# Wave 1's second half turned by DMA transposes, smaller first loads and later side work in an attention + MLP kernel

## The chip, the cores and the metric

One core of a Trainium2 chip runs the whole kernel. The metric is the device time in microseconds, as the median over runs. In the profile, PE is TensorE (matmuls), PEld its weight loads, DVE is VectorE, ACT is ScalarE, POOL is GpSimd and SP is SyncE, whose queue (SPq) issues nearly every DMA here. The sixteen DMA engines of the core serve that queue.

## The reference, cut to what matters

The input is q, k, v of shape (4 batches, 8 heads, 768 positions, 64), one decay factor `lam` for each head, and two weight matrices. The result is a decayed linear attention, followed by a two-layer MLP.

```python
for b in range(nb):                       # blocks of 64 positions
    intra = einsum('bhic,bhjc->bhij', qb, kb) * Dmask
    intra = einsum('bhij,bhjd->bhid', intra, vb)
    inter = einsum('bhid,bhde->bhie', qb * lam_pow, kv_state)
    out[:, :, sl] = intra + inter
    kv_state = lam_block * kv_state + einsum('bhsd,bhse->bhde', kb * rev_pow, vb)
x = out.transpose(0, 2, 1, 3).reshape(3072, 512)
h = x @ w_in                              # 512 -> 2048
g = h * (1 / (1 + exp(-1.702 * h)))
return g @ w_out                          # 2048 -> 512
```

## The kernel before, in words

The 3072 rows are worked through in six waves of 512 rows. Each wave runs an attention part (small matmuls), then `mlp1` with `gelu` (16 column groups `fc`, four matmuls of 128x512 each), then `mlp2` (four row groups of 16 matmuls each). All products are in bf16.

Waves 0 and 1 hold the first 256 positions of two batches each, and are built of eight units (bl, p): a batch and a pair of heads. Waves 2 to 5 hold 128 positions of all four batches and are built of four pairs p. The score matmuls need k and q with the head dimension on partitions, so both must be transposed after they have been scaled and cast. In waves 0 and 1, for each unit:

- `u_cast_kq` (L264) scales k on DVE and q on POOL from the f32 ring into `kqs`; `u_cast_v` (L270 on ACT, L272 on POOL) casts v.
- `u_turn` (L281) transposes with four PE matmuls against the identity into PSUM, and `u_turn_copy` (L289 on ACT, L291 on DVE) copies that to `kq`.
- `u_score` (L302), `u_mask` (L307), `u_kv0` (L327) with `u_kv0_copy` (L336), `u_inter` (L361) and `u_out` (L370) with a copy into `xT` (L372) do the rest; `u_state` (L348, L351) makes the state for wave 2.

In waves 2 to 5, `p_cast` (L382, L384) feeds a DMA transpose through the crossbar (L386) instead, and `p_out` sends its result through another one into `xT` (L436).

All inputs go through one SBUF `ring` of 52 half slots. A load is put on the list `coming`, and `pump()` issues from the head of that list as slots come free. Loads of waves 0 and 1 are `load_units` (L89, packets of 512 bytes), weights are `load_w` (L117), loads of wave 2 and later are `load_batch` (L101, packets of 256 bytes). SP issues in program order, and a DMA also waits until the eighth DMA before it has landed.

From wave 0's MLP on, the order of the instructions is written by hand on a virtual clock. `put` places the MLP work (`main`; one `fc` of 512 columns is 1, a half one is 0.5, four matmuls of `mlp2` are 1). `at` places attention work, casts and loads (`side`). A side item is emitted ahead of the first main item whose clock is not below its own. Each engine then works its instructions off in that order. `A_UNITS` is the first half of wave 1 (bl 0), done during wave 0's `mlp1`; `B_UNITS` is the second half (bl 1), done during wave 0's `mlp2`. `A_T` and `A_S` are the start and the step of the first half. `states`, `full` and `load_spread` place `u_state`, the attention of waves 2 to 5, and their loads.

Of the kernel before, what the change touches and what calls it, by code (L numbers as in the profile page):

```python
# [24 lines left out]
def kernel(  # L25
# [13 lines left out]
    nc = tc.nc  # L39
    f32 = mybir.dt.float32  # L40
    bf16 = mybir.dt.bfloat16
    B, H, S, D = q.shape
# [43 lines left out]
    def load_units(w, nm, bl, p, n=2):  # L86

        def go(x):
            nc.sync.dma_start(  # L89
                out=x.rearrange("s (h c) -> s h c", h=2 * n),  # L90
                in_=SRC[nm][2 * w + bl, 2 * p : 2 * (p + n), 0 : 2 * P, :].rearrange("h (q j) d -> q h (j d)", j=2))
            for i in range(n):
                loaded[w, nm, bl, p + i] = x.rearrange("s (n h j d) -> s n h j d", n=n, h=2, j=2)[:, i]
        coming.append((n, [(w, nm, bl, p + i) for i in range(n)], 1, go))

    def load_batch(w, nm, b):

        def go(x):
            if b == 0:
                loaded[w, nm] = x.rearrange("s (b p h d) -> s b p h d", b=B, h=2, d=D)  # L100
            nc.sync.dma_start(out=loaded[w, nm][:, b].rearrange("s p h d -> s (p h) d"),  # L101
                              in_=SRC[nm][b, :, w * P : (w + 1) * P, :].rearrange("h s d -> s h d"))
        coming.append((2 * B if b == 0 else 0, [(w, nm)] if b == 0 else [], NP, go))

    def load_batches(w):
        for nm in "kqv":
            for b in range(B):
                load_batch(w, nm, b)

    def load_w(kind, j, r):  # L110

        def go(x):
            if kind == "in":
                src = moe_w_in[r * P : (r + 1) * P, j * W : (j + 1) * W]
            else:
                src = moe_w_out[(j * CW + r) * P : (j * CW + r + 1) * P, :]
            nc.sync.dma_start(out=x, in_=src)  # L117
            loaded[kind, j, r] = x
        coming.append((2, [(kind, j, r)], 1, go))

    def pump():

        while coming:
            n, keys, reads, go = coming[0]
            i = (head[0] + (head[0] % 2 if n > 1 else 0)) % (2 * NR)
            if n == 0:
                coming.pop(0)
                go(None)
                continue
            if i + n > 2 * NR:  # L130
                i = 0
            if any(c in used for c in range(i, i + n)):
                break
            m = n // max(1, len(keys))
            for a, key in enumerate(keys):
                where[key] = [range(i + a * m, i + (a + 1) * m), reads]
            used.update(range(i, i + n))
            head[0] = i + n
            coming.pop(0)
            go(ring[:, i : i + n, :].rearrange("s n c -> s (n c)"))  # L140
# [17 lines left out]

    UNITS = [(bl, p) for g in range(2) for bl in range(2) for p in (2 * g, 2 * g + 1)]
    A_UNITS, B_UNITS = [(0, p) for p in range(NP)], [(1, p) for p in range(NP)]  # L160
    for p in (0, 2):
        for bl in range(2):
            for nm in "kqv":
                load_units(0, nm, bl, p)
    for u in ROWS:
        load_w("in", *u)
    for bl in range(2):
# [3 lines left out]
        if bl == 0:  # L171
            for u in ROWS:
                load_w("out", *u)
    load_batches(2)
    pump()

    zeros = const.tile([P, W], bf16)
# [65 lines left out]
    kqs_of, kq_of, sm_of = {}, {}, {}  # L243
# [40 lines left out]
    def u_turn_copy(w, bl, p, eng):  # L284
        if (w, p) not in kq_of:
            kq_of[w, p] = work.tile([P, 2, 2, 2, P], bf16, tag=f"kq{p}", name="kq")
        t, out = t_ps.pop((w, bl, p)), kq_of[w, p][:, bl]
        if eng is nc.scalar:
            nc.scalar.copy(out, t)  # L289
        else:  # L290
            eng.tensor_copy(out, t)  # L291

    s_ps = {}

# [215 lines left out]

    FILL0, FILL = 12, (0, 2, 2, 2, 1, 1, 1, 1)
    NF = 3
    A_T, A_S = 6, 1.4
    KV_ENG = {i: nc.vector if i in (2, 4, 6) else nc.scalar for i in range(1, 9)}

    with tc.manual_schedule():
# [8 lines left out]
        for i in range(N + 2):  # L525
            u = UNITS[i] if i < N else None
# [16 lines left out]
            if u:  # L543
                fill(FILL[i])
                u_turn(0, *u)
                u_turn_copy(0, *u, nc.vector if i < 2 else nc.scalar)
# [26 lines left out]
        def put(length, *item):  # L573
            main.append((clock[0], item))
            clock[0] += length

        def at(t, *item):
            side.append((t, item))

        def units1(t0, units, step, vcast, copier):  # L580
            n = len(units)
            for i in range(n + 2):
                t = t0 + step * i
                h = t + 0.5 * step
                if i < n:
                    at(t, u_cast_kq, 1, 0, *units[i], nc.vector)
                    at(t, u_cast_kq, 1, 1, *units[i], nc.gpsimd)
                    at(t, u_cast_v, 1, *units[i], vcast)
                if 0 < i:
                    at(h, new_o)  # L590
                if i < n:
                    at(h, u_turn, 1, *units[i])
                if i > 1:
                    at(h, u_inter, 1, *units[i - 2])
                if i < n:
                    at(h, u_turn_copy, 1, *units[i], copier)
                if 0 < i <= n:
                    at(h, u_score, 1, *units[i - 1])
                    at(h, u_mask, 1, *units[i - 1])
                    at(h, u_kv0, 1, *units[i - 1])  # L600
                if i > 1:
                    at(h, u_out, 1, *units[i - 2])
                if 0 < i <= n:
                    at(h, u_kv0_copy, 1, *units[i - 1], nc.scalar)

        def states(t0, w, step):
            for p in range(NP):
                at(t0 + step * p, u_state, w, p)

        def full(t_cast, t0, w, step, c_step=2.0):  # L610
            for p in range(NP):
                at(t_cast + c_step * p, p_cast, w, p)
            for p in range(NP + 1):
                t = t0 + step * p
                if p < NP:
                    at(t, p_score, w, p)
                    at(t, p_mask, w, p)
                if p:
                    at(t, p_inter, w, p - 1)
                    at(t, p_out, w, p - 1)  # L620
                if p < NP:
                    at(t, p_kv, w, p)

        def load_spread(t0, w, step):
            for i, nm in enumerate("kqv"):
                for b in range(B):
                    at(t0 + step * (B * i + b), load_batch, w, nm, b)
# [10 lines left out]
        for fc in range(3, FFC):  # L638
            put(0.5, fc_whole, 1, fc, HA)
        for n, u in enumerate(ROWS):  # L640
            at(13.2 + 0.6 * n, cast_w, "out", *u, nc.vector)
        e = clock[0]
        for j in range(NJ):
            for g in range(3):
# [1 line left out]
        for j in range(NJ):  # L646
            put(1, mlp2, 0, 3, j)
        states(e - 7, 0, 1.6)
        units1(e + 2, B_UNITS, 2, nc.scalar, nc.scalar)
        e = clock[0]  # L650
        for fc in range(FFC):
            put(0.5, fc_whole, 1, fc, HB)
        states(e + 0.5, 1, 1.5)
        for g in range(G):
            for j in range(NJ):
                put(1, mlp2, 1, g, j)
        full(e + 1, e + 7.6, 2, 2.4)
        load_spread(e + 4, 3, 1.8)
        for w in range(2, NW):
            e = clock[0]  # L660
# [47 lines left out]
```

## Time and profile before

| | |
|---|---|
| median of 13 runs | 220.68 us (220.04 to 221.97) |
| the profiled execution's own time | 221.12 us |
| its span | 219.3 us |
| PE busy | 211.2 us (96% of the span), 1766 matmuls |
| DVE, ACT, POOL busy | 106.1, 97.1, 28.8 us |
| DMA moved | 40.15 MB, mean 183 GB/s |
| DMA engines' busy share, five-us stretches from 5 to 60 us | 1.01 to 1.28 |
| the same from 60 to 75 us | 0.66 to 0.73 |

A busy share is a sum over packets of all sixteen engines and can pass 1 where packets overlap, so values of 1 and more mean a full queue. PE is busy in all of every five-us stretch from 45 us to the end of the MLP; its idle time lies ahead of that. The span of a matmul is longer than its share of the pipeline: 128x512 matmuls follow each other every 0.216 us, and one `fc` or four matmuls of `mlp2` take 0.86 us at the full clock.

### The profile page before, as it was taken

How to read it: one execution, taken by the hardware profiler on the slowest of the kernel's cores; microseconds unless marked ns; L12 is line 12 of the kernel's file. 1: busy time of each engine (PE TensorE's matmuls, PEld its weight loads, DVE VectorE, ACT ScalarE, POOL GpSimd, SP SyncE). 2: the span in 40 equal slices, each digit the busy share in tenths (PEclk: the TensorE clock that was granted, in tenths of full speed). 3: DMA queues.
4: the chain of work that ended last, by engine and by line, in shares of the span. 5: the costliest groups of instructions: out<-in, count | busy, mean ns of one | idle time of the engine just before them, and what ended most of it. 6: DMA issues, size and time to landing. Idle time of an engine off the chain costs nothing.

```text
span 219.3 us, 4494 instructions
## 1 busy us (share of the span) xinstructions
PE 211.2 (96%) x1766; PEld 108.7 (50%) x1766; DVE 106.1 (48%) x237; ACT 97.1 (44%) x203; POOL 28.8 (13%) x62
## 2 busy tenths in 40 slices
PE   7899969899999999999999999999999999999994
PEld 2464425575546755444554444544444444444453
DVE  3896536584415889182573295671393432100120
ACT  3786727774765612155621066611166520367000
POOL 4773051040040000004000040000040000000000
PEclk9999988999999999999999999999999999999999
DMA  4999999999965999899979979878974132200112
GB/s 120 296 328 371 333 308 388 361 270 216 221 126 126 168 213 212 179 249 219 228 155 179 234 170 190 170 155 176 236 155 85 34 88 75 96 0 0 48 51 96
DMA packets 96693, 40.15 MB, mean 183 GB/s; under 512 B 77088, under 2 KB 89632, under 8 KB 96672
## 3 DMA queue, kind: packets, MB, share of 16 engines
q1 hardware_dynamic: 96528, 39.86, 76.9%
q8 instruction: 14, 0.23, 0.5%
q14 instruction: 7, 0.06, 0.1%
q10 hardware_dynamic: 144, 0.00, 0.0%
HBM read 27.27 MB, written 6.29 MB: 153 GB/s over the span
## 4 chain that ended last, share of the span: by engine, by line
PE 84%; DMA 8%; SPq 5%; ACT 1%; issue 0%; POOL 0%; DVE 0%
PE ps_out L485 36%; PE ps_h L454 35%; DMA ring<-in_moe_w_in_dram 5%; SPq L89 4%; DMA ring<-in_q_dram 3%; PE ps_o L432 2%; PE ps_s L395 2%; PE ps_out L501 2%; PE ps_kv L410 1%; PE ps_o L425 1%; PE ps_t L281 1%; PE ps_kv L348 1%; PE ps_s L302 1%; SPq L117 1%; PE ps_o L370 0%
## 5 line engine op out<-in xcount | busy, mean ns | idle before, releaser
L454 PE MATMUL ps_h<-xT,w_in 128*128 128x512 bf16 (+1 forms) x448 | 89.1, 352 | 0.3 <-ACT g_sb L460 0.3
L460 ACT ACTIVATE g_sb<-ps_h 128x512 bf16<-128x512 f32 (+1 forms) x112 | 59.5, 536 | 61.2 <-PE ps_h L454 59.8
L485 PE MATMUL ps_out<-w_out,g_sb 128*128 128x512 bf16 x368 | 83.1, 379 | 0.0
L454 PEld LDWEIGHTS <-w_in 128*128 128x128 bf16 x448 | 42.3, 98 | 38.4 <-issue 1.6
L485 PEld LDWEIGHTS <-g_sb 128*128 128x128 bf16 x368 | 34.8, 98 | 38.9
L492 DVE COPY o_sb<-ps_out 128x512 f32<-128x512 f32 x19 | 13.1, 690 | 52.6 <-PE ps_out L485 49.8
L402 DVE SCALAR_TENSOR_TENSOR sm<-ps_s,inv_pow,mask 128x512 bf16<-128x512 f32 x32 | 22.6, 746 | 22.9 <-PE ps_s L395 22.8
L384 POOL CAST v_sb<-ring 128x512 bf16<-128x512 f32 x16 | 9.7, 650 | 103.4 <-DMA ring<-in_v_dram 67.6
L435 ACT CAST xs<-ps_o 128x512 bf16<-128x512 f32 x16 | 9.4, 586 | 29.2 <-PE ps_o L432 29.2
L307 DVE TENSOR_TENSOR sm<-ps_s,mask 128x512 bf16<-128x512 f32 x16 | 11.0, 688 | 11.3 <-PE ps_s L302 11.3
L264 POOL TENSOR_TENSOR kqs<-ring,kq_pow 128x256 bf16<-128x256 f32 x16 | 10.3, 658 | 28.7 <-DMA ring<-in_q_dram 25.1
L414 DVE SCALAR_TENSOR_TENSOR kv<-kv,blk,ps_kv 64x256 bf16<-64x256 bf16 x24 | 11.4, 476 | 0.2
L382 DVE TENSOR_SCALAR kqs<-ring,k_pow 128x256 bf16<-128x256 f32 x32 | 11.2, 390 | 0.2
L382 DVE TENSOR_SCALAR kqs<-ring,q_pow 128x256 bf16<-128x256 f32 x32 | 11.1, 388 | 0.0
L281 PE MATMUL ps_t<-ident,kqs 128*128 128x128 bf16 x64 | 7.1, 229 | 2.9 <-POOL kqs L264 1.9
L256 PE MATMUL ps_f<-zeros 128*128 128x512 bf16 x22 | 8.7, 520 | 1.3 <-DVE zeros L178 1.3
L264 DVE TENSOR_TENSOR kqs<-ring,kq_pow 128x256 bf16<-128x256 f32 x16 | 7.7, 492 | 3.3 <-ACT kq_pow L209 2.6
L281 PEld LDWEIGHTS <-kqs 128*128 128x128 bf16 x64 | 4.9, 102 | 8.0 <-DVE kqs L264 3.1
L289 ACT COPY kq<-ps_t 128x512 bf16<-128x512 bf16 x10 | 5.9, 587 | 6.2 <-PE ps_t L281 6.2
L351 DVE TENSOR_TENSOR kv<-kv_bd,ps_kv 64x128 bf16<-64x128 bf16 x16 | 4.6, 286 | 8.0 <-PE ps_kv L348 7.7
L372 ACT CAST xT<-ps_o 128x256 bf16<-128x256 f32 x16 | 6.0, 373 | 2.4 <-PE ps_o L370 2.1
L150 DVE CAST w_in<-ring 128x512 bf16<-128x512 f32 x13 | 5.4, 426 | 3.0 <-DMA ring<-in_moe_w_in_dram 3.0
(66 smaller groups left out, 119.3 us busy)
## 6 DMA issues: line engine op xcount, KB each, us to landing
ring<-in_k_dram SPq DMA_DIRECT2D x24, 256.0 KB, 5.0
ring<-in_q_dram SPq DMA_DIRECT2D x24, 256.0 KB, 4.9
ring<-in_v_dram SPq DMA_DIRECT2D x24, 256.0 KB, 4.5
ring<-in_moe_w_in_dram SPq DMA_DIRECT2D x16, 256.0 KB, 5.9
ring<-in_moe_w_out_dram SPq DMA_DIRECT2D x16, 256.0 KB, 5.3
out_dram<-o_sb SPq DMA_DIRECT2D x15, 256.0 KB, 2.2
out_dram<-o_sb SPq DMA_DIRECT2D x18, 128.0 KB, 2.5
kq<-kqs SPq DMA_TRANSPOSE x16, 3.3
```

The lines of the kernel that those rows point to most:

```text
L264: eng.tensor_tensor(kqs_of[w, p][:, bl, i].rearrange("s j h d -> s h j d"), read(w, "kq"[i], bl, p), tab, op=MUL)
L281: nc.tensor.transpose(t_ps[w, bl, p][:, i, j, :], kqs_of[w, p][:, bl, i, j].rearrange("s h d -> s (h d)"), ident)
L307: nc.vector.tensor_tensor(sm.rearrange("s h j t -> s h (j t)"), s_ps.pop((w, bl, p))[:, :, 0 : 2 * P], mask2.to_broadcast([P, 2, 2 * P]), ...
L382: nc.vector.tensor_scalar(kqs[:, i, :, h, :], x[:, :, p, h, :], scalar1=(k_pow, q_pow)[i][:, 2 * p + h : 2 * p + h + 1], scalar2=None, op0 ...
L384: nc.gpsimd.tensor_copy(v_sb[w % 2][:, p], read(w, "v")[:, :, p])
L402: nc.vector.scalar_tensor_tensor(sm[:, h], s[:, h], inv_pow[:, 2 * p + h : 2 * p + h + 1], mask.to_broadcast([P, B, P]), op0=MUL, op1=MUL)
L414: nc.vector.scalar_tensor_tensor(new[hd(h), p], old[hd(h), p], blk2[hd(h), p : p + 1], t[hd(h), :, hd(h)], op0=MUL, op1=ADD)
L435: nc.scalar.copy(xs.rearrange("s b h d -> s h b d"), o)
L454: nc.tensor.matmul(t[:, bs[0] * P : bs[1] * P], w_in_sb[fc // CW][:, kc, (fc % CW) * P : (fc % CW + 1) * P], xT(w)[:, kc, bs[0] : bs[1], : ...
L460: nc.scalar.activation(g_tile(w)[:, fc, c], h_ps.pop((w, fc))[:, c], GELU)
L485: nc.tensor.matmul(t, g_of[w][:, fc, g * P : (g + 1) * P], w_out_sb[j][:, fc % CW, :], start=(fc == 0), stop=(fc == FFC - 1))
L492: nc.vector.tensor_copy(o, t)
```

## The change

Five things are edited.

1. Wave 0's first loads are split: units (0,0) and (0,1) now have loads of 128 KB of their own. The rest keeps loads of 256 KB in the same order, so there are 15 loads in place of 12 for the same bytes.
2. The first half of wave 1 starts at clock 7 with step 1.2, in place of 6 and 1.4. The casts of `w_out` on DVE start at 12 with step 0.55, in place of 13.2 and 0.6.
3. The second half of wave 1 goes through a new `units1b`: no `u_turn` and no `u_turn_copy`, but `u_xbar`, a DMA transpose (128 KB) for each unit. All its v casts go to POOL, and its casts come earlier (from e-2.1, every 0.6).
4. Wave 2's loads are no longer appended at the start but placed on the clock. On SP's queue they come in this order: three k loads, crossbar 0, the fourth k load, crossbar 1, a q load, crossbar 2, a q load, crossbar 3, two q loads, four v loads.
5. The attention of wave 2 is placed two clock units earlier (e-1 and e+5.6 in place of e+1 and e+7.6).

```diff
-    for p in (0, 2):
-        for bl in range(2):
-            for nm in "kqv":
-                load_units(0, nm, bl, p)
+    for bl, p, n in [(0, 0, 1), (0, 1, 1), (1, 0, 2), (0, 2, 2), (1, 2, 2)]:
+        for nm in "kqv":
+            load_units(0, nm, bl, p, n)
...
-    load_batches(2)
     pump()
...
+    def u_xbar(w, bl, p):
+        nc.sync.dma_start_transpose(out=kq_of[w, p][:, bl].rearrange("p i j s -> p (i j) s"),
+                                    in_=kqs_of[w, p][:, bl].rearrange("p i j h d -> p (i j h d)"))
...
-    A_T, A_S = 6, 1.4
+    A_T, A_S = 7, 1.2
...
+        def units1b(t_cast, t0, c_step, step):
+            n = len(B_UNITS)
+            for i in range(n):
+                u = B_UNITS[i]
+                at(t_cast + c_step * i, u_cast_kq, 1, 0, *u, nc.vector)
+                at(t_cast + c_step * i, u_cast_kq, 1, 1, *u, nc.gpsimd)
+                at(t_cast + c_step * i, u_xbar, 1, *u)
+                at(t_cast + c_step * i, u_cast_v, 1, *u, nc.gpsimd)
+            for i in range(n + 1):
+                t = t0 + step * i
+                at(t, new_o)
+                if i < n:
+                    at(t, u_score, 1, *B_UNITS[i])
+                    at(t, u_mask, 1, *B_UNITS[i])
+                if i:
+                    at(t, u_inter, 1, *B_UNITS[i - 1])
+                if i < n:
+                    at(t, u_kv0, 1, *B_UNITS[i])
+                if i:
+                    at(t, u_out, 1, *B_UNITS[i - 1])
+                if i < n:
+                    at(t, u_kv0_copy, 1, *B_UNITS[i], nc.scalar)
...
-            at(13.2 + 0.6 * n, cast_w, "out", *u, nc.vector)
+            at(12 + 0.55 * n, cast_w, "out", *u, nc.vector)
...
-        units1(e + 2, B_UNITS, 2, nc.scalar, nc.scalar)
+        for b in range(3):
+            at(e - 3, load_batch, 2, "k", b)
+        units1b(e - 2.1, e + 3, 0.6, 1.8)
+        at(e - 1.6, load_batch, 2, "k", 3)
+        for b in range(B):
+            at(e - 1 + 0.6 * b, load_batch, 2, "q", b)
+            at(e + 3 + 1.2 * b, load_batch, 2, "v", b)
...
-        full(e + 1, e + 7.6, 2, 2.4)
+        full(e - 1, e + 5.6, 2, 2.4)
```

More of the change, by code (lines that the diff above doesn't have):

```diff
@@ L103, in load_batch @@
         coming.append((2 * B if b == 0 else 0, [(w, nm)] if b == 0 else [], NP, go))
-    def load_batches(w):
-        for nm in "kqv":
-            for b in range(B):
-                load_batch(w, nm, b)
     def load_w(kind, j, r):
@@ L160 @@
     A_UNITS, B_UNITS = [(0, p) for p in range(NP)], [(1, p) for p in range(NP)]
-    for p in (0, 2):
-        for bl in range(2):
-            for nm in "kqv":
-                load_units(0, nm, bl, p)
+    for bl, p, n in [(0, 0, 1), (0, 1, 1), (1, 0, 2), (0, 2, 2), (1, 2, 2)]:
+        for nm in "kqv":
+            load_units(0, nm, bl, p, n)
     for u in ROWS:
```

## The prediction

> **What bounds the kernel now.** I read the chain of waits first.
>
> ```profile
> PE 84%; DMA 8%; SPq 5%; ACT 1%; issue 0%; POOL 0%; DVE 0%
> ```
>
> TensorE sets the end, except for 13% that belongs to the loads. So a change counts if it removes PE work, or PE's idle time, or time at a lowered clock. PE's own list of waits says where it idles:
>
> ```profile
> PE ps_t L281 <- POOL kqs L264: 1.9, 3, 0.8
> PE ps_t L281 <- DVE kqs L264: 1.0, 1, 1.0
> ```
>
> Of these, 1.0 and 0.8 us stand at the first turn of wave 1, which waits for its k and q loads; the same chain in order of time has the place, and also the second half of wave 1 (start, us, what):
>
> ```profile
> 23.64 5.59 DMA ring<-in_q_dram
> ...
> 29.30 0.62 POOL kqs L264
> ...
> 29.98 0.28 PE ps_t L281 x2
> 30.26 2.73 PE ps_h L454 x8
> ...
> 49.87 2.59 PE ps_out L485 x12
> 52.46 0.22 PE ps_t L281 x4
> 52.69 1.73 PE ps_out L485 x8
> 54.41 0.22 PE ps_t L281 x4
> 54.63 0.24 PE ps_s L302 x8
> ```
>
> Eight matmuls at 30.26 take 2.73 us, where eight at 52.69 take 1.73. The view by stretches of time (stretch, length, then PE's busy time first, and the granted clock behind POOL) says why:
>
> ```profile
> 6.93:10.34 3.41, 2.50 (x39) 1.46 (x39) 2.71 (x6) 2.49 (x7) 2.81 (x6) 1.00 1.16 289
> 27.41:30.82 3.41, 1.61 (x11) 0.61 (x9) 1.37 (x4) 0.85 (x2) 1.28 (x3) 1.00 1.12 293
> 30.82:34.24 3.42, 3.42 (x23) 1.52 (x22) 1.37 (x3) 1.40 (x3) 2.77 (x6) 0.50 0.99 346
> ```
>
> PE was busy for 1.61 of 3.41 us, and then ran 3.42 us at half clock, which lost 1.71 us. A stretch with 2.50 us busy had no such sequel. The threshold lies between 0.9 and 1.8 us of idle time in such a stretch. From 45 us on PE never idles: what is lost there later is lost for good.
>
> **The change part by part.** The sum goes against the profiled execution: 221.12 us, with a span of 219.3. That is 0.44 us above the median of the runs (220.68); I make the sum of differences and put it on the median.
>
> Smaller first loads: three more issues of about 0.5 us each on SP, the same bytes. PE's early waits may shrink by up to 0.5 us, but PE then meets the wait at 28 us, whose k and q are last in a full DMA queue (share above 1). I take 0, hidden by that wait; without this cover it would be -0.5 to 0.
>
> Later start of the first half: one more `fc` (0.86 us) stands ahead of the first turn. PE comes there at 27.89 + 0.86 = 28.75, and k's cast lets it turn at 28.86; q's still only at 29.98. The idle time falls from 1.8 to 0.11 + 0.83 = 0.94 us, at the harmless end of the bounds above. So PE gains 0.86, and likely the 1.71 of the half clock too. The closer step costs something: only one `fc` stands between the first turns, and DVE's copy, mask and cast (0.42, 0.69, 0.42) for one unit hardly fit into it. I allow 0.7 us of new short waits (bounds 0 and 1.3). PE then reaches the next place, the end of the first twelve `mlp2` matmuls, at 52.46 - 0.86 - 1.71 + 0.7 = 50.6 us; the bounds are 49.9 and 52.46.
>
> No turns in the second half: sixteen PE transposes go, four pieces of 0.22 us in the chain: -0.88. ACT loses four copies of 0.59 and four v casts of 0.40, POOL gains four of about 0.45; neither is on the path.
>
> The crossbars are the new wait. In the changed order, PE runs twelve `mlp2` matmuls and then at once the first score, whose `kq` comes from crossbar 0. On SP's queue that crossbar stands behind the six loads of the second half and three k loads of wave 2. SP's timeline and the DMA issues (the last number is us from issue to landing) price it:
>
> ```profile
> 44.24 5.48 SPq L101 DMA_DIRECT2D ring<-in_k_dram  x4
> ...
> 47.08 1.53 SPq L101 DMA_DIRECT2D ring<-in_k_dram  x1
> ...
> 82.72 0.58 SPq L101 DMA_DIRECT2D ring<-in_q_dram  x1
> 83.41 1.32 SPq L436 DMA_TRANSPOSE xT<-xs  x1
> ```
>
> ```profile
> ring<-in_k_dram SPq DMA_DIRECT2D x1, 256.0 KB, 5.5
> ...
> ring<-in_q_dram SPq DMA_DIRECT2D x1, 256.0 KB, 3.4
> ...
> xT<-xs SPq DMA_TRANSPOSE x1, 3.3
> DMA to landing us min/median/max: 2.4/3.3/4.1
> ```
>
> The first of these lines holds all four k loads of wave 2, the second the third of them: issued at 47.08, landed at 47.08 + 5.5 = 52.6. A crossbar of this very shape behind a load (issued 82.72 and 83.41) landed 86.7 against 86.1, so 0.6 us after it. Crossbar 0 can be issued at 48.6, when SP is done with that k load; its casts are no later: q's load lands by 45.5, and DVE's k cast stands behind the state adds, which end by 48.9 even without a gain. It lands at 52.6 + 0.6 = 53.2. Bounds: 48.6 + 2.4 = 51.0 if it needn't wait for the queue, 48.6 + 6.2 = 54.8 if it takes as long as the slowest load there. I take 53.2, since the crossbar in that row also stood in a queue of loads.
>
> A page of the Trainium skill makes a crossbar transpose as fast as an ordinary transfer (Advanced Engine Details and Errata, X-Bar Transpose (TRN2)); by its 350 to 400 GB/s, 128 KB would be an estimated 0.35 us in place of the row's 0.6, and the landing 0.25 us earlier.
>
> So PE waits at the first score from 50.6 to 53.2, 2.6 us, for a load queue that is full from the start and that no gain of PE makes faster. All that was won before is absorbed here. Before, PE stood at 52.46 with the same work ahead plus four turns. Hence 53.2 - 52.46 - 0.88 = -0.14 us. On top comes the clock: an idle time of 2.6 us puts 1.3 us or more into one 3.41 us stretch, wherever the stretch begins, and 1.8 did it before. I take one drop, +1.71; the bounds are 0 and 1.71. Sum: +1.57.
>
> The rule of TensorE: Matmul & The Clock Gate (Part 1, HAM oscillation) speaks of idle gaps of more than about 3.4 us, by which a gap of 2.6 us would cost no clock and the sum would stay at -0.14. The row of 27.41 us, with 1.80 us idle and half clock after it, speaks against it, and I go by the row.
>
> Behind the first score nothing more should wait: each further load and crossbar adds 1.2 + 0.6 us to the queue (crossbar 1 at 55.0, 2 at 56.8, 3 at 58.6), while PE asks every 2.2 us (from 53.2: 55.4, 57.6, 59.8), later still at half clock. Behind the crossbars on SP stand wave 2's q and v loads; v lands some 2.4 us later than before (62.9, where POOL's wait for it ended), and is used after 72. Wave 2's earlier placement: its crossbars have five us and more before their scores. Earlier `w_out` casts fill DVE's idle time. All 0; without that cover a crossbar late by 1 us costs 1 us.
>
> **The rivals.** (1) Crossbar 0 does gate PE, but the clock stays: the split over two stretches is mild, or PE still drops at 30 us and so arrives late, with 1 us left to wait. -0.14, so 220.5. For it: 0.94 us idle plus new waits at 30 us is within the unknown band. Against: 2.6 us can't be split below 1.3. (2) The other side, faster: the crossbar doesn't stand behind the k loads, or those land early, and PE finds `kq` nearly ready. With a landing at 51.0 the wait is 0.4 us and the sum 51.0 - 52.46 - 0.88 = -2.34, so 218.3; it is faster from the point where crossbar 0 lands before 52.9 and the clock holds. For it: some crossbars landed 2.4 us after issue. Against: those stood in a queue with room (share 0.74 from 110 to 115 us, against 1.2 here). (3) The later crossbars are late as well: SP spends about 1.4 us on issuing each and up to 1.9 on a load in a full queue; 0.7 us more at two scores gives 223.7. (4) The change does nothing: excluded for the turns, which are gone from PE's order.
>
> **How the numbers follow.** Forecast, a wait at the first score and a clock drop: 220.68 + 1.57 = 222.25, chance 0.56, own range 221.4 to 223.0. Rival 1: 0.15. Rival 2: 0.22, spread from 218.3 to 220.2. Rival 3: 0.07. The range reaches down into rival 2 until about 0.12 is left below, and up to just short of rival 3: 219.4 to 223.4. About 0.2% (0.44 us) is what a measurement can tell from no change. Rival 1 falls within it for 0.09, and 0.03 to each side. Faster: 0.22 + 0.03 = 0.25; same 0.09; slower 0.56 + 0.07 + 0.03 = 0.66.
>
> **What would show it.** PE waits for a DMA that writes `kq` ahead of the score line, at 50 to 53 us, by 2 to 3 us; a stretch at 0.50 follows; crossbar 0 lands within 0.4 to 0.7 us after the third k load; the stretch at 31 us runs at 1.00, and PE's idle time at 28 us is 0.9. Wrong would be: crossbar 0 at or before 51 us, no half clock after the wait, or a gap at the later scores.

## The result and the profile after

The changed kernel takes 222.52 us in the median of 11 runs (221.68 to 226.38); the kernel before, measured beside it, takes 220.50 us (48 runs, 219.53 to 221.97). The ratio is 1.0084, with a 95% interval of 1.0066 to 1.0102: slower by 0.7 to 1.0%. The ratios here and below leave out runs more than 1.5% above the fastest of the same kernel, such as the one of 226.38 us; the medians include them. The forecast was 222.25 us, so the direction and the size came out right. The profiled execution took 222.05 us with a span of 220.3, 1.0 us more than the 219.3 before.

The chain of waits of the changed kernel, by engine:

```profile
PE 74%; DMA 17%; SPq 6%; issue 1%; POOL 0%; ACT 0%
```

Loads and crossbars (DMA and SPq) hold 23% of the chain. Before they held 13%, but 19% in a second profile of the kernel before, so this share says little. PE's own list of waits (total us, times, longest) names the new one:

```profile
PE ps_t L274 <- POOL kqs L257: 1.6, 2, 0.8
PE ps_s L300 <- DMA kq<-kqs: 1.4, 1, 1.4
PE ps_f L249 <- DVE zeros L171: 1.3, 1, 1.3
```

The chain in order of time (start, us, what) has its place, and SP's timeline (start, us, queue, line, operation) what stood ahead of it:

```profile
49.66 3.33 DMA kq<-kqs
53.00 0.04 issue
53.04 0.31 PE ps_s L300 x8
53.34 0.11 PE ps_o L325 x4
53.45 1.83 PE ps_out L483 x8
55.29 0.24 PE ps_s L300 x8
55.52 0.16 PE ps_o L359
...
56.03 1.83 PE ps_out L483 x8
...
67.72 0.44 PE ps_h L452 x4
```

```profile
45.18 4.05 SPq L101 DMA_DIRECT2D ring<-in_k_dram  x3
49.66 1.36 SPq L288 DMA_TRANSPOSE kq<-kqs  x1
51.08 0.56 SPq L101 DMA_DIRECT2D ring<-in_k_dram  x1
51.76 1.20 SPq L288 DMA_TRANSPOSE kq<-kqs  x1
```

The third of the k loads, with its place on SP's timeline and its time from issue to landing:

```profile
47.67 1.56 SPq L101 DMA_DIRECT2D ring<-in_k_dram  x1
...
ring<-in_k_dram SPq DMA_DIRECT2D x1, 256.0 KB, 4.8
```

It lands at 47.67 + 4.8 = 52.47. Crossbar 0 goes out at 49.66, behind three k loads and after DVE's cast of its k, which ends at 49.59. It lands at 53.00; PE has waited for it since 51.68. The later scores don't wait. The stretch after the wait, which the prediction expected at half clock, ran at full clock, as did the one with the wait in it (columns as in the prediction: stretch, length, busy time of PE, PEld, DVE, ACT and POOL, granted clock, DMA share, GB/s):

```profile
51.23:54.64 3.41, 2.05 (x21) 0.86 (x19) 1.89 (x4) 0.62 (x2) 0.25 (x1) 1.00 0.91 167
54.64:58.06 3.42, 3.42 (x41) 1.47 (x39) 0.69 (x1) 0.99 (x3) 0.00 (x0) 1.00 1.00 218
```

### The profile page after: what moved, and what is told of

Read it like the earlier page. It is cut to its first block, busy times and chain, and to the rows that moved or that the text cites. A ratio compares the mean times of both kernels' runs of the same rounds, so it can differ in the third digit from the quotient of the medians.

```text
span 220.3 us, 4462 instructions
## 1 busy us (share of the span) xinstructions
PE 210.3 (95%) x1750; PEld 107.4 (49%) x1750; DVE 108.0 (49%) x237; ACT 93.7 (43%) x195; POOL 30.8 (14%) x66
## 4 chain that ended last, share of the span: by engine, by line
PE 74%; DMA 17%; SPq 6%; issue 1%; POOL 0%; ACT 0%
PE ps_out L483 35%; PE ps_h L452 28%; SPq L89 6%; DMA ring<-in_moe_w_in_dram 5%; DMA ring<-in_moe_w_out_dram 5%; DMA ring<-in_q_dram 3%; PE ps_o L430 2%; PE ps_s L393 2%; DMA ring<-in_v_dram 2%; PE ps_out L499 2%; DMA kq<-kqs 2%; PE ps_kv L408 1%; PE ps_o L423 1%; PE ps_s L300 0%; PE ps_kv L346 0%
## 5 line engine op out<-in xcount | busy, mean ns | idle before, releaser
L452 PE MATMUL ps_h<-xT,w_in 128*128 128x512 bf16 (+1 forms) x448 | 88.1, 349 | 0.3 <-ACT g_sb L458 0.3
L382 POOL CAST v_sb<-ring 128x512 bf16<-128x512 f32 x16 | 9.5, 637 | 102.0 <-DMA ring<-in_v_dram 54.3
L380 DVE TENSOR_SCALAR kqs<-ring,k_pow 128x256 bf16<-128x256 f32 x32 | 11.3, 395 | 0.2
L380 DVE TENSOR_SCALAR kqs<-ring,q_pow 128x256 bf16<-128x256 f32 x32 | 11.1, 390 | 0.1
L257 DVE TENSOR_TENSOR kqs<-ring,kq_pow 128x256 bf16<-128x256 f32 x16 | 8.5, 533 | 3.4 <-ACT kq_pow L202 1.7
L349 DVE TENSOR_TENSOR kv<-kv_bd,ps_kv 64x128 bf16<-64x128 bf16 x16 | 4.6, 286 | 8.4 <-PE ps_kv L346 8.1
L274 PE MATMUL ps_t<-ident,kqs 128*128 128x128 bf16 x48 | 5.3, 228 | 2.8 <-POOL kqs L257 1.6
L265 POOL CAST v_sb<-ring 128x256 bf16<-128x256 f32 x16 | 7.5, 485 | 0.7 <-DMA ring<-in_v_dram 0.5
L145 DVE CAST w_out<-ring 128x512 bf16<-128x512 f32 x16 | 7.4, 504 | 0.1
```

What stands on the lines that cost most here:

```text
L145: eng.tensor_copy((w_in_sb if kind == "in" else w_out_sb)[j][:, r, :], read(kind, j, r))
L257: eng.tensor_tensor(kqs_of[w, p][:, bl, i].rearrange("s j h d -> s h j d"), read(w, "kq"[i], bl, p), tab, op=MUL)
L380: nc.vector.tensor_scalar(kqs[:, i, :, h, :], x[:, :, p, h, :], scalar1=(k_pow, q_pow)[i][:, 2 * p + h : 2 * p + h + 1], scalar2=None, op0 ...
L382: nc.gpsimd.tensor_copy(v_sb[w % 2][:, p], read(w, "v")[:, :, p])
L452: nc.tensor.matmul(t[:, bs[0] * P : bs[1] * P], w_in_sb[fc // CW][:, kc, (fc % CW) * P : (fc % CW + 1) * P], xT(w)[:, kc, bs[0] : bs[1], : ...
```

## The experiments

Twelve runs follow, in four groups; those of one group share a chip and the runs of the kernel before. Since the time to the first `mlp1` matmul varies by up to 1.7 us between the profiled executions (17.3 to 19.0 us, in kernels that load in the same way), the stages are compared by their lengths:

| kernel | median, us | ratio to before, 95% interval | wave 0's mlp1 to wave 1's | wave 1's to wave 2's | wave 2's to the end |
|---|---|---|---|---|---|
| before | 220.50 | | 49.4 | 26.45 | 125.7 |
| before, again | 220.75 | 0.9992 (0.9968 to 1.0015) | 48.9 | 26.46 | 126.1 |
| changed | 222.52 | 1.0084 (1.0066 to 1.0102) | 49.8 | 26.83 | 126.0 |
| changed, again | 221.92 | 1.0068 (1.0043 to 1.0093) | 49.5 | 26.82 | 126.0 |
| edits 1 and 2 alone | 219.92 | 1.0001 (0.9976 to 1.0026) | 48.5 | 26.46 | 125.8 |
| all but the crossbars | 220.66 | 1.0001 (0.9978 to 1.0024) | 48.1 | 26.83 | 125.8 |
| k loads behind the crossbars | 222.00 | 1.0077 (1.0056 to 1.0098) | 49.0 | 27.72 | 125.9 |
| inter first | 221.92 | 1.0073 (1.0044 to 1.0101) | 50.5 | 26.82 | 126.0 |
| old place of the first half | 221.88 | 1.0060 (1.0037 to 1.0083) | 48.4 | 26.83 | 126.0 |
| four k loads ahead | 223.96 | 1.0125 (1.0084 to 1.0165) | 50.8 | 26.81 | 126.0 |
| wave 2 in its old place | 222.73 | 1.0099 (1.0066 to 1.0132) | 49.6 | 26.46 | 127.3 |
| filler matmuls | 222.31 | 1.0070 (1.0043 to 1.0098) | 49.8 | 26.97 | 126.0 |
| crossbars on ScalarE's queue | 225.19 | 1.0182 (1.0133 to 1.0231) | 54.3 | 26.82 | 126.0 |
| the same, inter first | 224.05 | 1.0108 (1.0072 to 1.0144) | 51.2 | 26.83 | 126.2 |

The stages are taken from PE's timeline, from the first matmul of one wave's `mlp1` to that of another's, in one profiled execution each. (In the chains, `mlp1` of wave 1 or 2 begins 0.16 us later than on that timeline.) The loss lies in the first stage, where kernels with edits 1 and 2 and no crossbars need 48.1 to 48.5 us, the kernel before 48.9 without a half clock, and the changed one 49.5 to 49.8; 0.37 us of it lies in the second. (The old place of the first half has 48.4 because that execution started late, at 19.0, after a stretch at half clock from 11.1 us, and the crossbar held it at the same time as the others.)

**Edits 1 and 2 alone** (smaller first loads, later first half and earlier `w_out` casts, on the kernel before):

```diff
-    for p in (0, 2):
-        for bl in range(2):
-            for nm in "kqv":
-                load_units(0, nm, bl, p)
+    for bl, p, n in [(0, 0, 1), (0, 1, 1), (1, 0, 2), (0, 2, 2), (1, 2, 2)]:
+        for nm in "kqv":
+            load_units(0, nm, bl, p, n)
...
-    A_T, A_S = 6, 1.4
+    A_T, A_S = 7, 1.2
...
-            at(13.2 + 0.6 * n, cast_w, "out", *u, nc.vector)
+            at(12 + 0.55 * n, cast_w, "out", *u, nc.vector)
```

> The kernel before with only the split first loads, the later and closer first half of wave 1 and the earlier w_out casts; the second half still turns on PE. Theory (the crossbar took the gain of these edits away): PE ends the first twelve mlp2 matmuls near 51.7 us, as in the changed kernel, in place of 52.5, with no half clock at 31 us, and nothing takes it back: 219.7 us, about 0.8 below the kernel before. Rival (these edits bring nothing or cost, through the new short waits between the closer units): 220.5 us or more.

The profile had no half clock, and its second half began with the turn at 51.12 us, in place of 52.46. The median was 219.92 us beside 220.34 for the kernel before, but the ratio's interval holds 1. So these edits gain or lose at most a quarter of a per cent (0.9976 to 1.0026), not the 0.8 us expected; the loss is in the rest.

**The k loads behind the crossbars** (one load behind each, none ahead):

```diff
-        for b in range(3):
-            at(e - 3, load_batch, 2, "k", b)
...
-        at(e - 1.6, load_batch, 2, "k", 3)
         for b in range(B):
-            at(e - 1 + 0.6 * b, load_batch, 2, "q", b)
+            at(e - 2.05 + 0.6 * b, load_batch, 2, "k", b)
+        for b in range(B):
+            at(e - 0.2 + 0.6 * b, load_batch, 2, "q", b)
```

> The changed kernel with wave 2's k loads put one behind each crossbar, none ahead. Theory (crossbar 0 lands late because it stands behind three k loads): it lands about half a us behind the last load of the second half, by 50.5 us, PE's wait of 1.36 us at the first score is gone, and the time falls by 1.2 to 1.5 us, to about 221.1. Rival (a crossbar waits for its casts or takes its time in any order; the loads ahead don't matter): the wait stays above 1 us, time unchanged at 222.5.

```profile
49.05 1.30 SPq L288 DMA_TRANSPOSE kq<-kqs  x1
...
kq<-kqs SPq DMA_TRANSPOSE x1, 2.5
```

Crossbar 0 was issued at 49.05, when DVE's cast of its k had ended (48.99), and landed at 51.59, 2.54 us later. That is later than the expected 50.5, but the wait at the first score was gone. Wave 1's `mlp1` began at 66.61 us in the chain, 1.1 earlier than in the changed kernel's first profile. But the time did not fall as expected: the median lies between the two of the changed kernel. The chain of this kernel shows why:

```profile
67.29 1.43 PE ps_h L452 x12
...
69.85 0.83 DVE kqs L380 x2
...
70.86 1.31 DVE kqs L380 x2
72.17 0.03 issue
72.20 0.28 DVE kv L349
...
72.86 0.32 PE ps_kv L346 x8
```

Wave 2's casts (`kqs` L380) stand on DVE ahead of the state's adds (`kv` L349) on which PE waits (0.8 us in its list). The loads now land later (the last v at 69.3 in place of 66.9 us), so POOL casts v from 69.57 on, at the same time as DVE casts k and q:

```profile
69.57 2.46 POOL L382 CAST v_sb<-ring 128x512 bf16<-128x512 f32 x4 [18.28 <-DMA out_dram<-o_sb]
```

DVE's four casts then take 1.09 and 1.31 us for each two, where they take 0.62 and 0.61 in the changed kernel, whose v casts are done at 69.50, ahead of them. That they share something with POOL's casts is not shown beyond this overlap. What was won at one end of the load queue was paid at the other: the stage to wave 2's `mlp1` is 0.9 us longer.

**Inter first** (`u_inter` ahead of `u_score` in `units1b`, as `units1` had it):

```diff
+                if i:
+                    at(t, u_inter, 1, *B_UNITS[i - 1])
                 if i < n:
                     at(t, u_score, 1, *B_UNITS[i])
                     at(t, u_mask, 1, *B_UNITS[i])
-                if i:
-                    at(t, u_inter, 1, *B_UNITS[i - 1])
```

> The changed kernel with u_inter put ahead of u_score in each step of the second half (inter, score, kv0, out, as it stood before behind the turn). In the changed order a unit takes as long as before though its turn is gone: the pieces from score to out are 0.74 us, before 0.52 without the turn. Theory (the change between matmuls on the whole array and matmuls on quarters costs about 0.1 us each time, and the changed order has two more of them): four units gain about 0.2 each, 0.6 to 0.8 us in all, about 221.8. Rival (the time is the same in any order, the turn was hidden before): 222.5.

This run shows two things. The first is in its chain:

```profile
52.84 0.31 PE ps_s L300 x8
53.14 0.11 PE ps_o L325 x4
53.25 3.20 PE ps_out L483 x8
...
59.05 0.06 PE ps_o L359
59.11 0.24 PE ps_s L300 x8
...
59.57 1.83 PE ps_out L483 x8
```

From 59.05 to 59.57 one unit's small matmuls take 0.52 us; the same matmuls in the changed kernel take 0.74 (55.29 to 56.03), and in the kernel before they took 0.74 with a turn of 0.22 among them. In the changed kernel `inter` alone took 0.16 in place of 0.06. So the order score, inter, kv0 gave back what the turns had saved. The second is the 3.20 us of the first eight `ps_out`: this execution dropped to half clock after the wait.

```profile
50.14:53.56 3.42, 1.58 (x18) 0.66 (x17) 1.75 (x4) 0.26 (x1) 0.77 (x2) 1.00 0.97 180
53.56:56.97 3.41, 3.41 (x27) 1.40 (x26) 0.33 (x2) 0.35 (x2) 0.00 (x0) 0.50 0.87 186
```

From the first score to wave 1's `mlp1` it needed 68.46 - 52.84 = 15.62 us. Without the half of 3.41 that the clock took, that is 13.91, against 14.68 in the changed kernel. The median doesn't show these 0.77 us: it is 221.92, with an interval that overlaps that of the changed kernel. One of the six executions, the profiled one, had a drop.

**The old place of the first half** (edit 2 undone):

```diff
-    A_T, A_S = 7, 1.2
+    A_T, A_S = 6, 1.4
...
-            at(12 + 0.55 * n, cast_w, "out", *u, nc.vector)
+            at(13.2 + 0.6 * n, cast_w, "out", *u, nc.vector)
```

> The changed kernel with the old placement of wave 1's first half and of the w_out casts (6, 1.4 and 13.2, 0.6), the crossbars kept. Theory (the first score waits for crossbar 0, whose landing does not depend on PE): PE comes later by up to 0.8 us and waits that much less, the first score stays at 53.0 us, and the time stays at 222.5 within 0.4. Rival (the placement counts by itself): slower by 0.8 us or more.

221.88 us (ratio 1.006, 1.0037 to 1.0083). The first score stood at 52.85, behind a wait of 1.7 us for a crossbar that landed at 52.80. This profiled execution began its first `mlp1` 1.3 us later than that of the changed kernel, and the first score was not later: what decides is the time of the crossbar, not that of PE. PE was there at 51.14, no later than in the changed kernel with its later first half (51.68 and 51.1).

**Four k loads ahead**, in place of three:

```diff
-        for b in range(3):
+        for b in range(4):
             at(e - 3, load_batch, 2, "k", b)
...
-        at(e - 1.6, load_batch, 2, "k", 3)
```

> The changed kernel with the fourth k load also ahead of crossbar 0 (four loads ahead in place of three); nothing else is moved. Theory (the first score is pinned by crossbar 0, which lands behind the loads put ahead of it in SP's queue): one more load ahead delays crossbar 0 from 53.0 us to 54.5 to 55.0 us, the wait ahead of the first score of the second half grows from 1.4 to 2.9 to 3.4 us, and the time is 1 to 2 us above the changed kernel (about 223.5 to 224.5 us), more where the longer wait lets the clock drop. Rival (the loss lies in the second half's score units and in wave 2's earlier placement, and the wait at the first score is covered by slack behind it): crossbar 0 is later by as much, but the time stays within 0.4 us of the changed kernel.

The median rose to 223.96, 2.0 us above the changed kernel on the same chip; by the ratios to the kernel before (1.0125 and 1.0068) it is 1.3 us. In the profile, crossbar 0 came 1.1 us later than in the changed kernel beside it (52.71), at 53.80 and not at the expected 54.5 or later. The wait grew from 1.6 to 2.7 us, and wave 1's `mlp1` began 1.1 us later (68.53 against 67.44). Lines of the list of waits and of the chain:

```profile
PE ps_s L300 <- DMA kq<-kqs: 2.7, 1, 2.7
```

```profile
49.94 3.85 DMA kq<-kqs
53.80 0.04 issue
53.84 0.31 PE ps_s L300 x8
```

The wait reaches the end in full, as the theory had it; nothing behind it gives slack. The profile accounts for 1.1 us, nearly all of what the ratios show, and it ran at full clock. Four of this kernel's six executions had a mean clock of 0.992 or less, as one stretch at half clock makes it (3.41 / 2 of 220 us); of the changed kernel's 24, five. But the two kernels without crossbars and with edits 1 and 2 had three of twelve each. That is as often as the changed kernel, so its wait of 1.4 to 1.6 us adds no drops that these counts can show. A mean clock does not say where a drop was.

**Wave 2 in its old place**, two clock units later:

```diff
-        full(e - 1, e + 5.6, 2, 2.4)
+        full(e + 1, e + 7.6, 2, 2.4)
```

> The changed kernel with wave 2's attention put back to its old place (its casts and scores 2 us later in the hand-written order). Theory (the earlier placement costs the 0.37 us by which the stretch from the second half's first mlp1 to wave 2's first mlp1 is longer in the changed kernel, 26.83 against 26.46 us): the time falls by 0.3 to 0.5 us. Rival (the longer stretch comes from the late casts of the loads behind the crossbars, not from the placement): no change within 0.2 us.

The theory's 0.37 us are there (26.46 us in the table, in place of 26.82), but 1.3 us are lost in the next stage, and the median rose by 0.8 (the intervals overlap, and five of eleven executions had a mean clock of 0.992 or less). Wave 2's `mlp1` begins and then stands still. SP's timeline has the cause:

```profile
86.42 2.56 SPq L434 DMA_TRANSPOSE xT<-xs  x1
```

and the chain its end:

```profile
91.62 3.77 DMA xT<-xs
95.39 0.04 issue
95.43 4.69 PE ps_h L452 x21
```

In the old place the transposes into `xT` meet wave 3's q loads and the stores on SP's queue; the last landed at 95.39, and PE waited 1.2 us for it. The same wait was 0.2 us in the second profile of the kernel before. So with the crossbars and the later loads of wave 2, this profile loses more by the old placement than it gains.

**Filler matmuls** (six of 128x512 on zeros ahead of the first score):

```diff
+        def keep_busy(n):
+            t = ps.tile([P, W], f32, tag="t", bufs=1, name="ps_f")
+            for _ in range(n):
+                nc.tensor.matmul(t, zeros[:, 0:P], zeros, start=True, stop=True)
+
+        at(e + 2.99, keep_busy, 6)
```

> The changed kernel with six 128x512 matmuls on zeros (about 1.3 us on TensorE, results not used) put just ahead of the first score of the second half, where TensorE otherwise waits 1.4 us for crossbar 0. Theory (in some executions the wait lets the clock drop for some 3 us, as in the profile with inter first, and those executions make the median 0.5 us higher than the profile): the wait shrinks to 0.1 to 0.4 us, the clock is full around 53 to 57 us, and the median falls by 0.3 to 0.8 us. Rival (the wait costs its own length alone): the median is the same within 0.2 us or higher by what the fillers reach past crossbar 0's landing.

222.31 us (ratio 1.007, 1.0043 to 1.0098), beside 221.92 for the changed kernel. The wait shrank to 0.9 us, not to the expected 0.1 to 0.4, and the median did not fall. So nothing here shows that clock drops behind this wait set it. One of the seven executions had a mean clock of 0.992.

**The changed kernel again**:

> The changed kernel once more, beside the runs that take single parts of it away, so that they are compared on one chip. Theory (the profiled execution's order of waits is typical): 222.0 to 222.6 us, the first score again at 52.8 to 53.3 us behind crossbar 0, TensorE waiting 1.2 to 1.8 us for it. Rival (the loss comes from a state of that one chip): 220.5 us here, with crossbar 0 landing before TensorE needs it.

221.92 us (12 runs, 221.18 to 223.68), just below the expected range: wait 1.6 us, crossbar 0 at 52.71, first score at 52.75.

**The crossbars on ScalarE's queue**, and the same **with inter first**:

```diff
-        nc.sync.dma_start_transpose(out=kq_of[w, p][:, bl].rearrange("p i j s -> p (i j) s"),
+        nc.scalar.dma_start_transpose(out=kq_of[w, p][:, bl].rearrange("p i j s -> p (i j) s"),
...
```

> The changed kernel with its four crossbar transposes of the second half issued from ScalarE's queue in place of SP's; SP's loads of wave 2 keep their order and no longer have crossbars between them. Theory (crossbar 0 is late because it stands behind three loads in SP's queue, and with the crossbars moved off it the loads land no later than in the kernel before): crossbar 0 lands between 51.0 and 52.2 us, the wait ahead of the first score falls from 1.4 to 1.6 us to at most 0.5 us, wave 2's casts are not late, and the time falls by 0.8 to 1.5 us, to 220.5 to 221.2 us. Rival (the 16 DMA engines are full, and the queue a transfer stands in matters little): crossbar 0 lands at 52.7 to 53.3 us as before and the time stays within 0.3 us of the changed kernel, or rises by the 1.2 us per crossbar that ScalarE now spends on issuing while the gelus behind wait.

> The same, with inter also ahead of score in each unit of the second half, so that the small 64x64 matmuls stand together. Theory (the turn's saving of 0.88 us is real, but the order score, inter, kv0 gives back about 0.15 us in each of five units): 0.6 to 0.8 us below the kernel with the crossbars on ScalarE's queue, 219.8 to 220.5 us. Rival (what is gained ahead of wave 2's first mlp1 is waited for again there, as it was with the k loads behind the crossbars): within 0.2 us of the kernel with the crossbars on ScalarE's queue.

225.19 us (ratio 1.0182, 1.0133 to 1.0231) and 224.05 us (1.0108, 1.0072 to 1.0144). The theory fell twice. Crossbar 0 landed at 54.62 and 54.07 us, although it was issued at 48.90 and 48.62 from a queue with no load in it: 0.3 and 0.6 us behind the fourth k load, which SP had issued just before. So a queue of its own did not free it; both landings fit that it stands behind what was issued ahead of it on either queue. And ScalarE, which now waited for the casts before it could issue and then spent 2.24 us on the issue, held its gelus back (issue to landing of crossbar 0, and ScalarE's timeline, in the first of the two; the brackets give its idle time before and what ended it):

```profile
kq<-kqs ACTq DMA_TRANSPOSE x1, 5.7
...
48.90 2.24 ACTq L288 DMA_TRANSPOSE kq<-kqs  x1
51.19 0.39 ACT L458 ACTIVATE g_sb<-ps_h 128x256 bf16<-128x256 f32 x1 [4.11 <-DVE kqs L257]
```

PE waited 3.3 us for that gelu, and then ran the next twelve `ps_out` at half clock for most of the way (4.44 us in place of 2.59 in the chain). Its first score came at 57.35, after crossbar 0, so this run can't show what an early crossbar would give. Five of this kernel's six executions, and eight of the eleven with inter first, had a mean clock of 0.992 or less. With inter first, the stretch from the first score to wave 1's `mlp1` was 13.93 us in place of 14.62: again 0.7 us for the order.

**The kernel before again**:

> The kernel before once more, for a second profile of it: the first one holds a stretch at half clock (30.82 to 34.24 us) that may be no property of the kernel. Theory (it is in few executions): this profile shows full clock from 28 to 36 us, the second half's first turn starts at 51.0 to 52.0 us in place of 52.46 us, and the changed kernel's loss is larger in the profiles than the 1.0 us between the two spans. Rival: the half clock is there again, and the profiled executions can be compared as they are.

220.79 us in the profile, 220.75 in the median. The stretch at 30 us ran at full clock:

```profile
27.02:30.43 3.41, 2.05 (x13) 0.79 (x12) 1.53 (x4) 1.09 (x2) 1.47 (x3) 1.00 1.13 309
30.43:33.84 3.41, 2.85 (x30) 1.39 (x28) 2.18 (x4) 2.42 (x5) 2.77 (x6) 1.00 1.06 360
```

Of 79 executions of the kernel before that ran beside the experiments, five had a mean clock of 0.992 or less. The profile on which the prediction stood was one of the few.

**All but the crossbars** (edits 1 and 2, and wave 2's earlier place):

```diff
-        full(e + 1, e + 7.6, 2, 2.4)
+        full(e - 1, e + 5.6, 2, 2.4)
```

> The changed kernel without its third edit: the smaller first loads, the later first half and the earlier place of wave 2's attention stay, the second half is transposed on TensorE again, and wave 2's twelve loads go out in one piece as in the kernel before. Theory (the loss lies in the crossbars and the loads around them): no wait for a crossbar ahead of the second half, its first turn at 51.0 to 51.8 us, and 219.6 to 220.4 us, 1.7 to 2.5 us below the changed kernel; if the xT crossbars were near the path in the old place, up to 0.4 us below the kernel with the first two edits alone. Rival (the earlier place of wave 2's attention costs 0.37 us in itself): 220.2 to 220.6 us, above the kernel with the first two edits alone, and the stretch from the second half's first mlp1 to wave 2's first is 26.8 us in place of 26.46 us.

The shown edit is on top of edits 1 and 2. 220.66 us (12 runs, 219.59 to 222.13), 1.3 to 1.9 us below the two medians of the changed kernel, 0.7 to 0.8% by the ratios: that is what the crossbars and the loads around them cost. It lies just above both expected ranges; this execution began its first `mlp1` 0.8 us later than the changed kernel, and its first turn stood at 51.96. The stretch from wave 1's `mlp1` to wave 2's is 93.61 - 66.78 = 26.83 us, as in the changed kernel. So the rival's 0.37 us belong to the earlier placement itself. The chain shows where:

```profile
75.85 0.08 issue
75.93 0.40 PE ps_s L394 x8
...
76.83 0.38 PE ps_kv L409 x4
...
79.80 0.33 PE ps_s L394 x8
...
80.59 0.22 PE ps_kv L409 x4
```

The first lines are wave 2's second pair, which now follows `mlp1` matmuls: its score and its state take 0.40 and 0.38 us, with gaps of 0.08 and 0.03 ahead of them. Those of the third pair take 0.33 and 0.22 without such gaps, as the second pair's do in the kernel before. That is 0.34 of the 0.37.

No version beats the kernel before by more than the measurement can tell.

## Why the prediction was right, and where it was not

*Crossbar 0 is the new wait.* Right. It was put at 53.2 us, the third k load's 52.6 plus 0.6; it landed at 53.00, the load at 52.47. In the six kernels with three k loads ahead on SP's queue it went out between 48.67 and 49.66 and landed 0.53 to 0.65 us behind the third of them each time. The later crossbars were put at 55.0, 56.8 and 58.6 and landed at 54.9, 56.8 and 58.7, and no later score waited, as predicted. Four k loads ahead moved the landing and the end by the same 1.1 us, none ahead took the wait away, and an earlier or later PE changed nothing at the first score. The reason "on SP's queue that crossbar stands behind" was too narrow: on ScalarE's queue it landed behind the same loads. The Trainium skill has, on the page DMA: Bandwidth & Descriptors (Issuing engines are not separate DMA queues), that transfers run on the same sixteen DMA engines and interleave, whichever engine starts them. The 5.7 and 5.5 us of crossbar 0 on ScalarE's queue agree with it. Wave 2's last v load was mis-sized: it landed at 66.89 in place of 62.71, 4.2 us later and not 2.4. PE did not wait for it in the changed kernel, but it had little room left, as the run with the k loads behind shows.

*PE waits 2.6 us there.* The size was off: 1.4 and 1.6. PE was put at 50.6 and came at 51.68 and 51.1, since the denser first half costs more than the 0.7 us allowed for new short waits (with no clock drop and no new waits it would have been at 52.46 - 0.86 - 1.71 = 49.9, so they came to 1.8 and 1.2 us). The base has its part in this: the two kernels with the first half in its old place that ran at full clock there, the kernel before again and the old place, had PE at this point at 51.04 and 51.14. So these profiles show none of the 0.86 us of the later start. PE's later arrival moved nothing in the sum, which counts from the landing, but it made the wait shorter.

*"I take one drop, +1.71."* This step failed. It rests on a threshold, "between 0.9 and 1.8 us of idle time", that was read from one profile, and the runs show no such threshold (last section). Neither profile of the changed kernel has a drop there, and "no half clock after the wait" is one of the prediction's own signs of being wrong. Fillers in the wait did not lower the median. With the wait at 1.4 to 1.6 us, five of 24 executions of the changed kernel had a drop anywhere, and so had six of 24 of the two kernels without crossbars. With 2.7 us it was four of six; behind ScalarE, with waits of 3.3 and 2.5 us in the profiles, five of six and eight of eleven. These counts don't say where the drops were. They fit that longer waits bring more drops and that this wait was too short, but they don't show it: the profiled execution with 2.7 us had no drop. The skill's rule, idle gaps above some 3.4 us (TensorE: Matmul & The Clock Gate, HAM oscillation), doesn't describe these runs either: the drop after inter first followed a wait of 1.84 us.

*"No turns in the second half: -0.88."* Mis-sized in this kernel: first score to wave 1's `mlp1` takes 14.68 us, against 14.82 from the first turn in the kernel before, so the turns gave 0.14 (0.3 against the second profile of the kernel before). With inter first it is 13.91, so -0.91. The prediction costed the turns that went and not the `inter` that `units1b` moves behind the score.

*"Wave 2's earlier placement ... all 0."* Wrong by 0.37 us, which the run without crossbars shows as the placement's own cost; it also hides the `xT` transposes, which cost PE 1.2 us when the changed kernel has wave 2 in its old place.

*The sum.* Against the profile that the prediction used, the span rose by 1.0 us: first score 53.04 against the first turn's 52.46 is +0.58 (predicted +0.74), the shorter second half -0.14 (predicted -0.88), wave 2 +0.37 (predicted 0), the rest +0.2, and no clock drop (predicted +1.71). This adds up to +1.0, not to the predicted +1.57. The first of these terms was also read off an untypical base: in the second profile of the kernel before, without the half clock, the first turn ends its wait at 51.61, so that the same first score is 1.4 us later than that, and 1.1 in the second profile of the changed kernel. Against that base the terms are +1.4 for the first score, -0.3 for the second half, +0.4 for wave 2 and -0.1 for the rest, +1.4 in all. The medians differ by 2.0 us in the first comparison and by 1.0 in the later one. That the forecast came out within 0.3 us of the first is luck, since errors of both signs cancel: a clock drop was added that is rare, and a drop in the base, the order of the small matmuls and wave 2's place were left out. By mechanism it was rival 1, a crossbar that gates PE at full clock, which the prediction put at 220.5 us.

## What to carry to other kernels

Ahead of replacing compute with a transfer, look at what the DMA engines have been given by then: here a small transfer landed 0.3 to 0.7 us behind the load issued ahead of it, from another queue too, and loads put off to make room were missed later. When a step goes out of a sequence of small matmuls, look at what stands next to what afterwards. Take a second profile of the base ahead of pricing a stretch at a lowered clock.

## What the runs showed of the hardware

The half clock does not follow from PE's busy time alone. The next stretch ran at half clock after stretches of 3.41 us in which PE was busy for 1.08 us (ScalarE's queue), 1.58 (inter first), 1.61 (kernel before) and 1.80 (the old place of the first half, the first row below). It kept the full clock after 1.47 (four k loads, the second and third row) and 1.68 (ScalarE's queue, the last row):

```profile
7.66:11.07 3.41, 1.80 (x29) 0.93 (x30) 2.31 (x6) 1.35 (x4) 2.08 (x5) 1.00 1.10 304
...
49.72:53.14 3.42, 1.47 (x7) 0.49 (x5) 1.84 (x4) 0.00 (x0) 1.22 (x2) 1.00 1.15 200
53.14:56.55 3.41, 2.71 (x37) 1.33 (x39) 0.86 (x2) 0.62 (x2) 0.00 (x0) 1.00 0.77 160
...
46.64:50.05 3.41, 1.68 (x21) 1.34 (x21) 3.32 (x8) 0.39 (x2) 3.18 (x6) 1.00 1.22 234
```

So 1.95 us of idle time in a stretch cost no clock in one execution, and 1.61 did in another. The kind of matmul doesn't sort them either: the stretch with 1.08 us held only wide matmuls of the MLP and lost the clock, the one with 1.68 held small ones too and kept it. What decides stays open.

The small matmuls depend on their neighbours: a unit of the second half takes 0.52 us in the chain with `inter` ahead of the score and 0.74 with it behind, for the same matmuls. What in PE costs this was not measured.
